# One packed pair, whole-chunk masks, fixed PSUM pools and column sums on TensorE, in a fused linear-attention and MLP kernel

## The chip, the cores and the metric

The kernel runs on one core of a Trainium2 chip. The metric is the device time of one execution in microseconds (us). Inputs and the output are float32 in the chip's main memory (HBM); products on TensorE (PE) are taken in bf16. The other engines are VectorE (DVE), ScalarE (ACT) and GpSimd (POOL); the SyncE queue (SP) issues all transfers.

## The reference, cut to what matters

A recurrence over 768 steps for 4 batches x 8 heads of 48 channels, then a two-layer MLP over all 3072 tokens:

```python
for t in range(S):                                   # S = 768
    cur = einsum('bhd,bhe->bhde', u[None] * k_t, v_t)
    y[:, :, t] = einsum('bhd,bhde->bhe', r_t, state + cur)
    state = w_t[:, :, :, None] * state + einsum('bhd,bhe->bhde', k_t, v_t)
x = y.transpose(0, 2, 1, 3).reshape(B * S, H * D)    # 3072 x 384
g = s * max(x @ w_in, 0) ** 2 + b                    # w_in 384 x 2048
out = g @ w_out                                      # w_out 2048 x 384
```

## The kernel before, in words

**Attention.** The time axis is cut into chunks of 128 steps: 6 per batch, 24 in all, numbered n = 0 to 23, in an order that takes the first two chunks of each batch first. For each chunk the steps are:

- `load` brings w, r, k and v, 192 KB each, as runs of 192 bytes (48 floats). `ln` (ACT) takes log w.
- `cum` (PE, L357) multiplies log w by triangular matrices, which gives the cumulative sums: x = 0 the exclusive ones with the chunk's whole decay in four more columns, x = 1 the negative inclusive ones. From chunk 8 on (`ONE`) only x = 0 is made, and `inc` (DVE, L416) adds log w to it. `exp` and `exn` (ACT, L411 and L426) take exponentials into E.
- `mul` (DVE, L435 or L442) gives r and k scaled by E (`prd`). `tr` and `tev` transpose them: up to chunk 8 PE transposes and ACT copies out (L469, L489, L492); from chunk 9 on a DMA transpose issued from SP does both (L499).
- `mt` (PE, L529 or L541) makes the transposed scores of each head, and `msk` (DVE, L553) multiplies them by the causal mask into bf16.
- `dmm` (PE), `sup` (DVE) and `st` (POOL) bring the 48 x 48 states forward; `l2` (POOL) spreads the decay.
- `rkp`, `rku` (POOL), `cd` (DVE, L343) and `yd` (POOL, L349) give the diagonal term with u; `vb` casts v to bf16.
- `ymm` (PE, L572 to L604) forms y from scores and state, `yev` (DVE, L649) adds the diagonal term, and `xtr` (PE) and `xev` (ACT, L712) transpose the result into xT.

**Packed pairs.** The first two chunks of a batch can be loaded as a pair: each partition then gets two neighbouring steps, in runs of 384 bytes, and each "chunk" of the pair holds every second step. Such a pair needs more, smaller matmuls (two per cumulative sum, halves of 64 rows for scores and y) and its own masks. Before, `PK = 4`: two pairs, chunks 0 to 3.

**MLP.** Two chunks make a tile of 256 tokens, T = 0 to 11. `g1` (L747) makes h in eight pieces of six matmuls per tile, `relu` (ACT, L760) and `sq` (ACT L770 or DVE L772) give the activations, `g2` (L791) multiplies by w_out, in quarters of four matmuls, for each half of the tile, `oev` (DVE, L802) scales by s and adds the bias term, and `store` (SP, L821) writes out. The weights come in four pieces each (`li`, `lo`), cast to bf16 by `ci` and `co`.

**The bias term** is b times the column sums of w_out. Before, DVE adds the float32 pieces (`csred` L829, `csadd` L836), `cssplit` (L839, L840) splits the sum into two bf16 parts, `csspread` (PE, L847) sums them over partitions with a matrix of ones, and `csevac` (ACT, L853) scales by b.

**PSUM.** There are eight banks. Six form one pool `P`, which cums, transposes, scores, states, y, xT and h share, one bank per buffer, in rotation; two belong to the o products (`o`).

**Order.** Nothing is scheduled at run time. The string `ORDER` lists every operation, and each engine runs its own in this order; `@A`, `@D` or `@P` after a name puts it on another engine, and `+16` stands for 16 warm-up products on PE (L1117). The plan (`add`) only states dependences and buffers: a buffer's next user waits until the last reader of the user before it is done. The waits themselves are made when the kernel is built. Loads, DMA transposes and stores stand in one SP queue, so an operation that waits there holds up those behind it.

Of the kernel before, what the change touches and what calls it, by code (L numbers as in the profile page):

```python
# [8 lines left out]
FP32 = mybir.dt.float32  # L9
# [13 lines left out]
WB = 5  # L23
VB = 6
PK = 4
# [13 lines left out]
load0.0 ln0 load0.1 ln1 +16 cum0.0 exp0.0 cum0.1 cum1.0 load0.2 exp0.1 exp1.0 load2.0 load_u cum1.1  # L39
load0.3 l21 load2.3 load2.1 mul0.0 mul0.1 l20 +3 tr0 exp1.1 ln2 u_mm ln3 mul1.0 cum2.0 mul1.1 tev0  # L40
u_ev tr1 exp2.0 tev1 cum2.1 vb1@A exp2.1 rkp0 vb0 rku0 cd0 +6 mt0 msk0.0 load2.2 load4.0 msk1.0
cum3.0 dmm0 li0 exp3.0 sup0 st0 msk0.1 rkp1 cum3.1 li1 msk1.1 +7 dmm1 ymm0 ymm1 vb2 exp3.1 mul2.0
mul2.1 yd0 l22 li2 mul3.0 tr2 ln4 li3 rku1 vb3 cd1 mul3.1 rkp3 cum4.0 ci0 tr3 yd1 yev0 rku3 l23 sup1
yev1 +3 dmm2 tev2 xtr0 exp4.0 tev3 xev0 xtr1 sup2 cd3 lo0 xev1 rkp2 ci1 st2 st1 +3 mt2 dmm3 msk2.0
rku2 g10.0 l24 msk2.1 lo1 msk3.0 msk3.1 g10.1 sup3 ci2 relu0.1 g10.2 sq0.1 relu0.0 lo2 small2
relu0.2 small sq0.2@A sq0.0@A ci3 g10.3 yd3 lo3 cd2 ymm3 g10.4 yev3 yd2 ymm2 co0 g10.5 g10.6 load5.0
relu0.4 yev2 g20.0 sq0.4 co1 relu0.3 xtr2 relu0.6 relu0.5 xev2 xtr3 g10.7 cum4.1 xev3 csred0 g20.4
g11.0 g11.1 sq0.6@A sq0.5@A sq0.3@A csred1 load6.0 load4.1 load4.3 load4.2 g11.2 g11.3 g20.5 load5.1
co2 csadd1@D csred2 load5.2 co3 relu0.7 relu1.0 sq0.7@A relu1.1 relu1.2 exp4.1 sq1.0@A g20.6 load6.1
load6.2 csadd2@D csred3 ln5 g11.4 g20.1 g11.5 cum5.0 sq1.2 cum5.1 g11.6 sq1.1 g20.2 ln6 csadd3@D  # L50
exp5.0 relu1.3 load5.3 cum6.1 g20.3 load7.0 cssplit relu1.4 load8.0 csspread relu1.5 exp5.1 cum6.0
g20.7 load9.0 csevac mul4 sq1.3 oev0.0 tr4 relu1.6 exp6.0 mul5 vb4 dmm4 g21.0 g21.1 exp6.1 rkp4 rku4
tr5 sup4 st4 load6.3 vb5 load7.1 tev4 oev0.1 tev5 g11.7 relu1.7 l25 rkp5 load7.2 sq1.7 sq1.5 sq1.4
load7.3 rku5 load9.3 mul6 g21.4 mt4 ln7 load8.1 cd4 msk4.0 sq1.6 msk5.0 tr6 g21.5 dmm5 msk4.1 cum7.0
g21.6 l26 yd4 msk5.1 cd5 ymm4 tev6 ln8 sup5 g21.2 yev4 cum7.1 cum8.0 yd5 inc8 ymm5 ln9 load8.2 g21.3
exp7.0 vb6 xtr4 exp8.0 exp7.1 st3 l27 yev5 cum9.0 exn8 st5 mul7 oev1.0 xtr5 xev4 vb7 xev5 exp9.0
g21.7 load10.0 inc9 dmm6 g12.0 relu2.0 load11.0 sup6 rkp6 l28 sq2.0 g12.1 relu2.1 tr7 rku6 dmm7
load9.1 g12.2 tev7 sq2.1 sup7 relu2.2 g12.3 load9.2 g12.4 mul8 sq2.2 mt6 vb9@A relu2.3 rkp7 load10.1
g22.0 g12.5 sq2.3 relu2.4 g22.1 msk6.0 msk6.1 sq2.4 msk7.0 rku7 rkp8 load8.3 load12.0 l29 cd6
relu2.5 load10.2 yd6 exn9 cd7 msk7.1 oev1.1 ln10 sq2.5 ymm6 g12.6 relu2.6 yd7 ln11 yev6 g12.7 mul9  # L60
ymm7 tr8 cum10.0 g22.4 g22.5 g22.6 rku8 xtr6 yev7 inc10 xtr7 st7 tev8 load11.3 relu2.7 exp10.0 st6
sq2.7 xev6 xev7 g22.2 dmm9 cum11.0 sq2.6@A exn10 cd8 exp11.0 load11.1 sup9 inc11 g13.0 tev9 load13.0
vb8 l210 load10.3 store0.1 store0.0 rkp9 rku9 vb11 g13.1 load13.1 g13.2 mul10 g22.7 dmm8 relu3.0
relu3.1 sq3.0@A mt8 rkp10 g22.3 relu3.2 exn11 g13.3 sup8 msk8.0 msk9.0 cd9 g13.4 yd8 st8 ln12 sq3.1
relu3.3 sq3.3 ln13 vb10@A load11.2 msk8.1 g13.5 oev2.0 ymm8 cum12.0 yd9 relu3.5 load12.1 relu3.4
msk9.1 g23.0 sq3.4@A load13.2 exp12.0 oev2.1 ymm9 sq3.5@D g13.6 g23.4 dmm10 tev10 load12.2 rkp11
yev8 g13.7 cum13.0 l211 inc12 xtr8 rku10 yev9 exn12 st9 sq3.2 xev8 xtr9 rkp13 rku11 g23.1 g23.2
relu3.6 xev9 g23.5 relu3.7 mul11 load12.3 store1.0 sq3.6@A exp13.0 g23.6 tev11 sq3.7 inc13 cd10
load13.3 store1.1 sup10 g14.0 dmm11 g14.1 g14.2 relu4.0 mul12 st10 exn13 g14.3 sup11 cd11 relu4.1
mul13 relu4.2 load14.0 g23.3 g14.4 sq4.0@A relu4.3 sq4.1 sq4.2@A rku13 relu4.4 sq4.3 mt10 g14.5  # L70
g23.7 g14.6 msk10.0 msk10.1 oev3.0 ln14 relu4.5 rkp12 g14.7 load15.1 msk11.0 tev13 tev12 msk11.1
cum14.0 vb12 l212 rku12 yd10 ymm10 g24.0 yd11 oev3.1 ymm11 relu4.6 relu4.7 yev10 inc14 dmm12 yev11
sup12 sq4.7 xtr10 g24.4 g24.1 cd12 sq4.4@D xev10 exp14.0 cd13 load16.0 l213 xtr11 load15.0 mt12
g24.5 vb13@A sq4.5 load14.1 xev11 ln15 exn14 msk12.0 load17.1 msk12.1 g15.0 g24.6 msk13.0 g15.1 yd12
load14.2 st11 msk13.1 ymm12 st12 rkp14 relu5.0 cum15.0 dmm13 load15.2 ln16 yd13 mul14 rkp15 rku14
g15.2 sq4.6 inc15 sup13 g24.2 relu5.2 load17.0 relu5.1 sq5.0 yev12 load18.1 store2.0 g15.3 g24.3
exp15.0 cum16.0 g15.4 sq5.2 ln17 exn15 ymm13 load16.1 l214 g15.5 load14.3 sq5.1 relu5.3 relu5.4
g24.7 load16.2 store2.1 oev4.0 sq5.3 l215 vb14 load17.2 rkp17 rku15 inc16 yev13 xtr12 g25.0 exp16.0
g15.6 xtr13 tev14 relu5.5 st13 l216 mul15 oev4.1 relu5.6 exn16 tev15 load17.3 xev12 xev13 cum17.0
g15.7 exp17.0 dmm14 g25.1 relu5.7 g25.4 store3.1 store3.0 load15.3 g16.0 sq5.6@A sq5.5@D inc17 g16.1  # L80
sq5.4 g25.5 g16.2 cd14 cd15 sup14 g25.2 g16.3 relu6.1 g25.6 sq5.7 l217 vb17@P load20.0 mul16 st14
rku17 yd14 yd15 exn17 rkp16 load18.0 relu6.0 mul17 load16.3 load21.1 sq6.1 load18.3 load18.2
store4.1 relu6.2 sq6.0@A load19.0 relu6.3 mt14 msk14.0 tev17 sq6.2@A g16.4 tev16 g16.5 g25.3 msk15.0
vb15 ln18 msk14.1 oev5.0 msk15.1 g16.6 relu6.6 dmm15 relu6.4 g25.7 cum18.0 ymm14 sup15 load21.0
oev5.1 sq6.4 inc18 yev14 ymm15 g26.4 yev15 relu6.5 sq6.3 exp18.0 g26.0 g26.5 exn18 xtr15 sq6.5@D
g16.7 ln19 g26.6 xtr14 dmm17 store4.0 g26.1 xev14 load20.1 xev15 load19.1 relu6.7 g26.2 sq6.6@A
# [75 lines left out]
def kernel(  # L162
# [995 lines left out]
```

## Time and profile before

| | |
|---|---|
| median of 3 runs | 198.82 us (197.65 to 199.19) |
| the profiled execution: its time, its span | 198.82 us, 197.0 us |
| granted TensorE clock, mean over the span | 0.983 |
| h products (L747), 576 matmuls | 73.4 us busy |
| o products (L791), 400 matmuls | 74.3 us busy |
| masks (L553), 48 of 128x512 | 30.8 us busy |
| r and k products (L442, L435) | 30.3 us busy |
| relu (L760), 96 of 128x512 | 54.7 us busy, 21.4 us idle before it |
| column sums on DVE (L829, L836, L839, L840) | 10.3 us busy |
| DMA queue of SP | 113426 packets, 33.83 MB, 76.6% of 16 engines' span |

Busy times are unions of what the profiler recorded. PE's matmuls are pipelined and overlap, so the time that a piece takes on PE is better read from one piece's start to the next one's. In a line of the timeline, the first number is the start in us from the span's start, the second the time covered, then engine, line, operation, output and inputs, and in brackets the idle time of that engine just before and what ended it. "PEld" is the weight load, which overlaps PE.

### The profile page before, as it was taken

Reading aid. Unit: us, or ns where it says so; the run is one execution under the profiler, and the core shown is the slowest. Engines: PE = TensorE matmul, PEld = TensorE weight load, DVE = VectorE, ACT = ScalarE, POOL = GpSimd, SP = SyncE. Lnnn points to the kernel's source line nnn. Section 1 sums busy time; section 2 is a strip of 40 time slices with the busy share of each in tenths; the row PEclk is TensorE's granted clock in tenths of the full one; section 3 lists DMA queues with packets and bytes.
Section 4 is the critical chain, followed back from the end, with each engine's and each line's share of the span. In section 5 each row is a group of like instructions: output and inputs, shape, how many; then the busy total and the mean of one; then the engine's idle time right before and its main releaser. Section 6 shows DMA issues by size and latency. Waiting matters only on the chain.

```text
span 197.0 us, 5099 instructions
## 1 busy us (share of the span) xinstructions
PE 180.9 (92%) x1994; PEld 141.6 (72%) x1994; DVE 150.1 (76%) x260; ACT 137.1 (70%) x268; POOL 110.1 (56%) x147
## 2 busy tenths in 40 slices
PE   7898699978698988999998998999999999999992
PEld 4466488855468867868876886778787777789772
DVE  7469569999788995989989878859949699533222
ACT  3682956965538959978784886588888858366730
POOL 3686970168249499866859389539459456100000
PEclk9999889999969999999999999999999999999999
DMA  6999998979997009969898998998499981020023
GB/s 155 261 259 350 403 352 261 179 154 224 214 213 150 3 7 227 171 145 195 136 210 187 223 239 173 222 224 162 79 203 236 193 189 45 0 80 5 2 78 120
DMA packets 113449, 34.14 MB, mean 173 GB/s; under 512 B 108177, under 2 KB 111378, under 8 KB 113426
## 3 DMA queue, kind: packets, MB, share of 16 engines
q1 hardware_dynamic: 113426, 33.83, 76.6%
q8 instruction: 15, 0.25, 0.5%
q14 instruction: 8, 0.07, 0.1%
HBM read 25.17 MB, written 4.72 MB: 152 GB/s over the span
## 4 chain that ended last, share of the span: by engine, by line
PE 46%; DVE 19%; DMA 8%; issue 7%; SPq 7%; POOL 7%; ACT 4%; DVEq 0%; POOLq 0%; ACTq 0%
PE o_ps L791 19%; PE h_ps L747 18%; SPq L294 5%; DVE gT L772 4%; DMA vt<-in_v_dram 4%; DVE mt_sb L553 3%; DMA u_row<-in_u_dram 2%; POOL yd L349 2%; DVE wo_st L829 2%; DVE prd L442 2%; DMA rkt<-in_k_dram 2%; ACT RK L489 2%; SPq L302 2%; PE y_ps L604 1%; POOL rkp L320 1%
## 5 line engine op out<-in xcount | busy, mean ns | idle before, releaser
L791 PE MATMUL o_ps<-w_out,gT 128*128 128x384 bf16 (+1 forms) x400 | 74.3, 323 | 1.0 <-DVE gT L772 0.8
L747 PE MATMUL h_ps<-xT,w_in 128*128 128x256 bf16 x576 | 73.4, 275 | 1.5 <-ACT xT L712 1.3
L760 ACT ACTIVATE rh<-h_ps 128x512 bf16<-128x512 f32 x96 | 54.7, 601 | 21.4 <-PE h_ps L747 20.4
L747 PEld LDWEIGHTS <-w_in 128*128 128x128 bf16 x576 | 61.8, 114 | 6.1 <-issue 1.7
L791 PEld LDWEIGHTS <-gT 128*128 128x128 bf16 x400 | 37.2, 98 | 18.8 <-DVE gT L772 1.2
L770 ACT ACTIVATE gT<-rh 128x512 bf16<-128x512 bf16 x58 | 35.8, 640 | 0.3
L326 POOL TENSOR_TENSOR rku<-rkp,u_bc 128x384 f32<-128x384 f32 x24 | 26.4, 1099 | 4.4 <-DVE cd L343 4.0
L349 POOL TENSOR_TENSOR yd<-vt,cd 128x384 bf16<-128x384 f32 x20 | 18.1, 909 | 18.9 <-DVE cd L343 18.1
L442 DVE TENSOR_TENSOR prd<-rkt,E 128x768 bf16<-128x768 f32 x20 | 25.3, 1270 | 4.1 <-DMA rkt<-in_k_dram 3.6
L320 POOL TENSOR_TENSOR rkp<-rkt 128x384 f32<-128x384 f32 x20 | 23.6, 1183 | 8.0 <-DMA rkt<-in_k_dram 8.0
L772 DVE TENSOR_TENSOR gT<-rh 128x512 bf16<-128x512 bf16 x38 | 22.4, 600 | 7.2 <-ACT rh L760 7.1
L553 DVE TENSOR_TENSOR mt_sb<-mt_ps,tri_strict 128x512 bf16<-128x512 f32 x40 | 25.7, 680 | 1.3 <-PE mt_ps L541 1.2
L802 DVE SCALAR_TENSOR_TENSOR o_sb<-o_ps,s_bc,bconst 128x384 f32<-128x384 f32 (+1 forms) x25 | 14.8, 593 | 11.5 <-PE o_ps L791 11.5
L411 ACT ACTIVATE E<-cums 128x388 f32<-128x388 f32 (+1 forms) x32 | 15.6, 498 | 11.4 <-DVE inc L416 7.0
L686 POOL TENSOR_TENSOR st<-stmp,l 128x384 bf16<-128x384 bf16 x16 | 15.2, 955 | 5.9 <-DVE stmp L677 5.9
L870 POOL CAST vb<-vt 128x384 bf16<-128x384 f32 x16 | 9.0, 567 | 12.5 <-DMA vt<-in_v_dram 12.5
L649 DVE TENSOR_TENSOR x_sb<-y_ps,yd 128x384 bf16<-128x384 f32 x24 | 13.0, 548 | 3.2 <-PE y_ps L604 1.8
L416 DVE TENSOR_TENSOR inc<-cums,logw 128x384 f32<-128x384 f32 x16 | 8.8, 550 | 6.6 <-ACT E L411 4.3
L343 DVE TENSOR_REDUCE cd<-rku 128x8 f32<-128x384 f32 x24 | 12.7, 540 | 1.5 <-POOL rku L326 1.5
L712 ACT COPY xT<-xt_ps 128x384 bf16<-128x384 bf16 x24 | 10.7, 484 | 2.7 <-PE xt_ps L697 2.7
L315 ACT ACTIVATE logw<-wt 128x384 bf16<-128x384 f32 x20 | 10.3, 527 | 2.3 <-DMA wt<-in_w_dram 2.2
L677 DVE TENSOR_TENSOR stmp<-d_ps,st 128x384 bf16<-128x384 f32 x16 | 8.8, 547 | 1.5 <-PE d_ps L636 1.0
(94 smaller groups left out, 201.8 us busy)
## 6 DMA issues: line engine op xcount, KB each, us to landing
out_dram<-o_sb SPq DMA_DIRECT2D x23, 192.0 KB, 3.0
wt<-in_w_dram SPq DMA_DIRECT2D x20, 192.0 KB, 3.8
rkt<-in_r_dram SPq DMA_DIRECT2D x20, 192.0 KB, 4.0
vt<-in_v_dram SPq DMA_DIRECT2D x20, 192.0 KB, 3.6
rkt<-in_k_dram SPq DMA_DIRECT2D x20, 192.0 KB, 3.9
wi_st<-in_moe_w_in_dram SPq DMA_DIRECT2D x4, 768.0 KB, 8.0
wo_st<-in_moe_w_out_dram SPq DMA_DIRECT2D x4, 768.0 KB, 6.3
pkt<-in_w_dram SPq DMA_DIRECT2D x2, 384.0 KB, 4.8
```

Source lines behind the costliest of these rows:

```text
L320: nc.gpsimd.tensor_tensor(out=rkp, in0=c["r"], in1=c["k"], op=ALU.mult)
L326: nc.gpsimd.tensor_tensor(out=rku.rearrange("t h d -> t (h d)"), in0=c["rkp"].rearrange("t h d -> t (h d)"), in1=u_bc, op=ALU.mult,)
L349: nc.gpsimd.tensor_tensor(out=yd, in0=c["v"], in1=c["cd"].unsqueeze(2).to_broadcast([128, H, D]), op=ALU.mult,)
L411: nc.scalar.activation(out=c["E"][:, x, 0:w], in_=ps[:, 0:w], func=AF.Exp)
L442: nc.vector.tensor_tensor(out=prd[:, :, :, 0:D], in0=c["rk"], in1=c["E"][:, :, 0:HD].rearrange("t x (h d) -> t x h d", h=H), op=ALU.mult,)
L553: nc.vector.tensor_tensor(out=c["mt"][:, sg], in0=c["mt_ps"][sg], in1=(masks[:, n % 2] if packed(n) else tri_strict) .unsqueeze(1) .to_bro ...
L686: nc.gpsimd.tensor_tensor(out=c["st_new"], in0=c["stmp"].rearrange("q p (g e) -> q p g e", g=2), in1=c["l2"].unsqueeze(3).to_broadcast([12 ...
L747: nc.tensor.matmul(ps[:, f, :], lhsT=w_in_sb[ft // FPP][:, kt, :].rearrange("p (m j) -> p j m", j=FPP)[:, ft % FPP, :], rhs=xT[T][:, kt, : ...
L760: nc.scalar.activation(out=rh, in_=hs[T, i], func=AF.Relu)
L770: nc.scalar.activation(out=g, in_=rh, func=AF.Square)
L772: nc.vector.tensor_tensor(out=g, in0=rh, in1=rh, op=ALU.mult)
L791: nc.tensor.matmul(os_[T, k][:, cols], lhsT=gT[T][:, ft, tt * 128 : (tt + 1) * 128], rhs=w_out_sb[ft // FPP][:, ft % FPP, cols], start=(ft ...
```

## The change

It replaces the order string and, with it, five things:

1. `PK = 2`: one packed pair (chunks 0 and 1). Chunks 2 and 3 are loaded and computed like the rest; with one pair, the chunk order is batch 0's first two, then the first chunks of batches 1 to 3, then their second chunks, and so on. The packed transposes get two buffers (`RK2`).
2. PSUM: pool `P` is cut into `A`, one buffer of two banks for cums and scores; `B`, two buffers of one bank for transposes, states, y, xT and the column sums; and `h`, two of one bank. The pool `o` stays.
3. Both halves of a chunk's cumulative sum form one operation in one `A` buffer, read by one wide exponential and, up to chunk 7, a small one for the decay.
4. Scores and masks: one `mt` and one `msk` of 1024 columns per chunk, where there was one `mt` per two chunks and four `msk` of 512 columns. The masked scores have three buffers instead of four.
5. Column sums: 48 matmuls with one column of ones (`colsum`) add up w_out's bf16 pieces in a `B` buffer; DVE splits 128x3 values, and six matmuls spread them. The float32 pieces' staging buffers come free after their cast.

In the order, warm-up products are 74 instead of 38; four squares and five casts of v more are on ACT; of the w_in casts, piece 1 goes from POOL to ACT and piece 2 from ACT to DVE; load_u is third; and the loads of r and k for chunk 4 stand between the w_out pieces. The words that name the change speak of padded tiles; the padded tiles are in both kernels, but for `cs_sum`, which is 128x2x16 and used in three columns. `mul` of a packed chunk becomes one operation of two instructions.

```diff
-PK = 4
+PK = 2
-    psP = ctx.enter_context(
-        tc.tile_pool(name="psP", bufs=6, space=bass.MemoryType.PSUM)
+    psA = ctx.enter_context(
+        tc.tile_pool(name="psA", bufs=1, space=bass.MemoryType.PSUM)
     )
+    psB = ctx.enter_context(
+        tc.tile_pool(name="psB", bufs=2, space=bass.MemoryType.PSUM)
+    )
+    psH = ctx.enter_context(
+        tc.tile_pool(name="psH", bufs=2, space=bass.MemoryType.PSUM)
+    )
...
-    def cum(n, x):
+    def cum(n):
+        ps = psA.tile([128, 2, 512], FP32, name="cums", tag="A")
...
+        if n < ONE:
+            nc.scalar.activation(out=E[:, :, 0:HD], in_=ps[:, :, 0:HD], func=AF.Exp)
+            if cc < NCH - 1:
+                nc.scalar.activation(
+                    out=c["lam"], in_=ps[:, 0, HD : HD + HP], func=AF.Exp
+                )
+            return
...
     def mt(n):
-        two = [n, n + 1]
...
+        ps = psA.tile([128, 2, HP, 128], FP32, name="mt_ps", tag="A")
...
+    def mask(n):
+        m = work.tile([128, 2, HP, 128], BF16, name="mt_sb", tag="mt_sb")
         nc.vector.tensor_tensor(
-            out=c["mt"][:, sg],
-            in0=c["mt_ps"][sg],
+            out=m.rearrange("s g p t -> s (g p) t"),
+            in0=c["mt_ps"].rearrange("s g p t -> s (g p) t"),
...
-        ps = psP.tile([128, FPQ, TOK], FP32, name="h_ps", tag="P")
+        ps = psH.tile([128, FPQ, TOK], FP32, name="h_ps", tag="h")
...
-    def csred(i):
...
+    def colsum(i):
+        if i == 0:
+            os_["cs"] = psB.tile([128, 512], FP32, name="cs_ps", tag="B")
+        for ft in range(i * FPP, (i + 1) * FPP):
+            for kt in range(KT):
+                nc.tensor.matmul(
+                    os_["cs"][:, kt : kt + 1],
+                    lhsT=w_out_sb[i][:, ft % FPP, kt * 128 : (kt + 1) * 128],
+                    rhs=ones[:, 0:1],
+                    start=(ft == 0 and kt == 0),
+                    stop=(ft == FT - 1 and kt == KT - 1),
+                )
...
-        dict(w=WB, rk=8, v=VB, lw=NLW, prd=NPR, E=2, RK=RKB, M=MB, vb=6, yd=6, x=XSB, RK2=1,
-             cd=4, rkp=2, rku=2, l2=5, P=6, o=2, gT=3, xT=XTB, rh=4, inc=1,
+        dict(w=WB, rk=8, v=VB, lw=NLW, prd=NPR, E=2, RK=RKB, M=3, vb=6, yd=6, x=XSB,
+             cd=4, rkp=2, rku=2, l2=5, A=1, B=2, h=2, o=2, gT=3, xT=XTB, rh=4, inc=1,
```

The start of the new order, up to the first h product:

```text
load0.0 load0.1 load_u load0.2 load2.0 ln0 ln1 load2.1 +18 cum0 load2.2 u_mm exp0 load0.3 +2 cum1
l20 mul0 li0 exp1 rkp1 u_ev +1 tr0 load3.1 ln2 mul1 tev0 load3.2 +6 cum2 rku1 +2 tr1 exp2 load2.3
...
xtr0 yev1 xev0 +3 cum3 cd2 rku3 dmm2 xtr1 exp3 load4.0 sup2 +6 dmm1 xev1 mul3 lo0 ci1@A +2 ymm2
g10.0
```

## The prediction

> **What bounds the kernel now.** I read the whole span first (the page), then a table of five stretches, then waits and the order of time in each. The stretches are cut where TensorE's order changes: its first h product at 24.8 us, the first h product of tile 2 (g12.0) at 60.8, the last attention product at 166, the last matmul at 193.5.
>
> ```profile
> PE 180.9 (92%) x1994; PEld 141.6 (72%) x1994; DVE 150.1 (76%) x260; ACT 137.1 (70%) x268; POOL 110.1 (56%) x147
> ```
> ```profile
> core 0: us, PE busy (x) PEld busy (x) DVE busy (x) ACT busy (x) POOL busy (x), PEclk, DMA share, GB/s
> 0.00:24.80 24.80, 20.23 (x300) 13.78 (x300) 16.65 (x42) 15.12 (x24) 17.55 (x37) 0.96 1.06 287
> 24.80:60.80 36.00, 32.01 (x344) 24.06 (x344) 31.35 (x50) 23.10 (x46) 16.18 (x21) 0.93 0.95 221
> 60.80:166.00 105.20, 101.15 (x1112) 81.65 (x1112) 90.85 (x148) 83.45 (x170) 75.56 (x90) 1.00 0.83 168
> 166.00:193.50 27.50, 27.48 (x243) 22.08 (x240) 10.87 (x22) 15.42 (x30) 0.83 (x1) 1.00 0.10 36
> 193.50:197.00 3.50, 0.00 (x0) 0.00 (x0) 0.42 (x1) 0.00 (x0) 0.00 (x0) 1.00 0.35 123
> ```
>
> Until 24.8 loads and short chains bound it (DMA share 1.06). From 24.8 to 60.8 PE loses 4.0 us idle, and its clock is 0.93. From 60.8 on it is TensorE: 4.0 us idle in 105, none in the tail. To count losses I give each piece of PE work its start-to-start time when nothing waits: an h product of six matmuls 0.656 us (18 in 1.97 in the chain), an o quarter 0.65, and per chunk cum 0.27, score products 0.275, y 0.53, state 0.17, the x transpose 0.33, the transposes of r and k 0.45 where PE makes them. In the written order these sum to 29.5 us from the first h product to g12.0, and took 36.0: 6.5 lost. From there to the last matmul they sum to 131.8 and took 132.7: 0.9 lost. So the long stage has nothing to win on PE, and whatever makes PE wait there adds to the time.
>
> The waits of PE inside the second stretch, in order of time:
>
> ```profile
> 44.62 0.34 PE L847 MATMUL csb_ps<-cs_sum,ones 128*128 128x384 bf16 x1 [1.34 <-DVE cs_sum L839]
> 45.21 0.32 PE L847 MATMUL csb_ps<-cs_sum,ones 128*128 128x384 bf16 x1 [0.25 <-DVE cs_sum L840]
> ...
> 52.78 0.62 PE L469 MATMUL trps<-identity,prd 128*128 128x128 bf16 x8 [1.75 <-DVE prd L442]
> ```
>
> Two belong to the column sums, which leave; the third is the chain of chunk 6. The chain of waits runs through loads just before:
>
> ```profile
> 43.87 1.06 SPq L294
> ...
> 46.78 0.70 SPq L294
> 47.53 3.55 DMA vt<-in_v_dram
> ```
>
> Last, how long a result stays in PSUM until it is read out. The line with L541 makes the scores of chunks 8 and 9, the next three mask them; then a cumulative sum (L389) and its two readers:
>
> ```profile
> 78.06 0.62 PE L541 MATMUL mt_ps<-RK 48*128 48x128 bf16 x16
> ```
> ```profile
> 79.07 1.27 DVE L553 TENSOR_TENSOR mt_sb<-mt_ps,tri_strict 128x512 bf16<-128x512 f32 x2
> 80.72 0.68 DVE L553 TENSOR_TENSOR mt_sb<-mt_ps,tri_strict 128x512 bf16<-128x512 f32 x1
> 81.84 0.68 DVE L553 TENSOR_TENSOR mt_sb<-mt_ps,tri_strict 128x512 bf16<-128x512 f32 x1
> ```
> ```profile
> 85.13 0.33 PE L389 MATMUL cums<-logw,tri_strict 128*128 128x384 bf16 x1
> ```
> ```profile
> 88.00 0.52 ACT L411 ACTIVATE E<-cums 128x388 f32<-128x388 f32 x1
> ```
> ```profile
> 88.54 0.56 DVE L416 TENSOR_TENSOR inc<-cums,logw 128x384 f32<-128x384 f32 x1 [0.86 <-ACT E L411]
> ```
>
> The cumulative sum is held from 85.13 to 89.1, 4.0 us; over chunks 9 to 23 the hold is 1.6 to 4.2 us, mean 3.1. The first mask starts 0.4 to 2.7 us after the scores do (mean of ten pairs 1.14), and two masks take 1.36, so a chunk's scores are held about 2.5 us, 4.06 at the most. Before, six shared banks take this up. After, cums and mt_ps share one double bank, "A", used twice per chunk: 3.1 + 2.5 = 5.6 us of the 5.8 us that a chunk takes in the third stretch (105.2 us for 18 chunks).
>
> **The change part by part.** The profiled execution has a span of 197.0 us and a time of 198.82, 1.8 more, which is also the median of the three runs; I add 1.8 to spans. The padding that the change names stands in both kernels: what moves is everything else in the diff.
>
> 1. One packed pair instead of two. Loads: four of 384 KB go, eight of 192 KB come. In the busy queue packed loads are issued every 1.48 us (7.21, 8.70, 10.18), unpacked ones every 1.01 (25 from 36.10 to 61.37): 8 x 1.01 - 4 x 1.48 = +2.2 us of queue time. From the eight loads issued between 42.24 and 49.29 alone (0.88 each) it is +1.1. I take 2.2, the longer sample. It lies ahead of chunk 4 to 7's loads, which the chain runs through. The Trainium skill, "DMA: Bandwidth & Descriptors", sections "Why small descriptors are slow (HBM only)" and "How a descriptor splits into AXI transactions", counts beats of 32 B plus about 3 cycles per packet: 9 for a run of 192 B, 15 to 18 for one of 384. By it (an estimate) a packed load of 1.48 us becomes two of 0.74 to 0.89, and the price is 0 to 1.2 us, not 2.2; the time below would then be 201.6 to 202.8.
>
> 2. PE work. Up to the first h product the idle PE has warm-up products to spare (74 instead of 38, 0.11 us each); these cost only where they stand before ready work. From g10.0 to g12.0 the pieces sum to 30.3 instead of 29.5: two packed y products leave (0.92 each), chunk 3's front part comes in, and the column sums bring 48 one-column matmuls. Eight such (L378) take 0.29 us, four (L395) 0.10, so 1.2 to 1.7, taken 1.4. From g12.0 on it is 132.5 instead of 131.8, one o quarter more.
>
> 3. Column sums leave VectorE: eleven adds, a cast and a subtraction, 10.3 us busy between 32.8 and 45.2. Most lay beside a PE busy all of 30 to 40; the two waits above, 1.6 us, go. Their cover was missing only there.
>
> 4. Masks: 24 of 1024 columns for 48 of 512. From 384 columns (0.548) to 512 (0.68) a column costs 1.03 ns, so one takes 0.68 + 0.53 = 1.21 instead of 1.36; bounds 0.95 (a 768-column product at its shortest) and 1.36. VectorE gets 3.6 us lighter; beside a PE-bound stage that is worth nothing by itself. Four squares and five casts of v move to ACT (4 x 0.64 + 5 x 0.51 = 5.1 us); ACT is idle 60 us, so 0.
>
> 5. Start, walked along the new order. Both halves of cum0 come before exp0: 6.7 instead of 6.3. The u product now stands before cum1 on PE; u is loaded third, at about 1.9, and if it takes 4.8 us as now, PE is through it at 7.6. Then cum1 8.6, exp1 9.6, ln2 10.1, tev0 11.1, exp2 12.1, tev1 13.1, mt0 13.6 (now 12.95). With one buffer the masks go in turn: mask 0 to 15.0, mt1 15.5, mask 1 16.9, mt2 and cd0, mask 2 18.8, yev0 19.3, xtr0 19.7, xev0 20.3, exp3 21.3, xev1 21.8. The first h product starts at 21.8 instead of 24.8, because only chunk 2 goes ahead of it rather than a second packed pair, and because ACT no longer waits for the first weights ahead of tev2 (2.9 us idle at 16.4). Bounds: 19.8 (no u wait, no buffer turns) and 25 (the walk's waits on loads as long as now). Step: -3.0.
>
> 6. PSUM. For each use of A in the new order I take the PE work between the end of one user and the start of the next, 32 uses from g12.0 on, and compare it with the holds above less the piece's own PE time (2.8 after a cum, 2.2 after scores). Nine fall short, by 3.6 us in all, and 0.3 before g12.0. With the shortest holds (1.5 and 1.6 after the piece) none falls short: 0. With the longest everywhere (3.9 and 3.8) the sum is 27.4. The two "B" buffers (y, d, trps, xt; holds y 1.9, d 1.8 in the mean) fall short by 1.6 before g12.0 and 1.2 after. For h (two buffers) the work between a product and the next but one is never under 1.0 us; nine times it is 1.0 to 1.4, and a relu of 0.60 with its semaphores fits: 0 to 3.6, taken 0. After g12.0 I take 4.0 for A, B and h together, not 4.8, since a wait for A gives B its time too. That is nearest to the mean holds, which the same engines at nearly the same load will repeat. The Trainium skill, "Perfetto Trace Analysis", section "Matmuls", says that independent matmul groups should rotate through PSUM banks so that the read-out of one overlaps the next; by that rule a one-buffer A exposes the read-out at every use, which from these holds would be nearer the 27.4 than the 3.6, and the time as much as 227.
>
> Sum: first h product at 21.8; pieces 30.3; losses 6.5 - 1.6 + 2.2 + 1.6 + 0.3 = 9.0; g12.0 at 61.1, +0.3 against now. Then +0.7 of pieces and +4.0 of PSUM waits: 197.0 + 5.0 = 202.0, time **203.8 us**.
>
> **The rivals.** A, faster: the gain at the start is kept. For it: VectorE is 10 us lighter while it was on the chain, and the new order brings chunk 4's k ahead of two of the weight pieces. Without the 2.2 and the B waits g12.0 comes at 21.8 + 30.3 + 4.9 = 57.0, 3.8 early, and with no PSUM waits the end is 197.0 - 3.8 + 0.7 = 193.9, time 195.7. It decides where g12.0 is before 58 us and the waits after it are under 2 us. Against: the holds. B, no change: the start as in my sum, short holds later (0 to 2): 197.0 + 0.3 + 0.7 + 1 = 199.0, time 200.8 at its upper edge; with 1.1 for the loads 199.7. C, much slower: A is the bound. For it: 5.6 of 5.8 us. Halfway between the mean and the longest holds (15.5 in place of 3.6) the time is 203.8 + 11.9 = 215.7; a third of the way, 207.8. Against: the order was laid out for these gaps, and PE waits slow the work that crowds VectorE. That the change does little is part of B: PE work differs by 1.5 us only.
>
> **How the numbers follow.** Forecast (200.8 to 208) 0.50, A 0.18, B 0.19, C above 208 0.13. Within 1% is about what a measurement of this kernel can tell from no change. Faster 0.18, same 0.19, slower 0.63. The range leaves a tenth on each side: 196.5, above A's 195.7, to 210, in C's near part. The likeliest case's own range is 200.8 to 208.
>
> **What would show it.** The first h product near 21.8; g12.0 near 61; PE waits, named by exp, inc or mask, in front of cum and mt after it, some 3 to 5 us; no PE wait for relu over 0.5 us; the bias product with no wait for VectorE. Wrong would be: g12.0 before 58 (A), idle PE over 10 us after it (C), or PE waits for DMA.

## The result and the profile after

| | before | after |
|---|---|---|
| median | 198.73 us (4 runs, 197.65 to 199.19) | 188.09 us (4 runs, 187.63 to 188.47) |
| profiled execution: time, span | 198.82, 197.0 | 188.43, 186.7 |
| granted clock, mean | 0.983 | 0.999 |
| first h product (g10.0), that of tile 2 (g12.0) | 24.79, 60.83 | 22.13, 53.46 |

The ratio of the times is 0.947 (95% interval 0.942 to 0.952): 10.6 us faster, where 203.8 was forecast. First the line of the page with busy time by engine, then the same five stretches, cut at the same places of the order:

```profile
PE 180.7 (97%) x1994; PEld 142.3 (76%) x1994; DVE 131.7 (71%) x220; ACT 142.0 (76%) x277; POOL 104.5 (56%) x141
```
```profile
core 0: us, PE busy (x) PEld busy (x) DVE busy (x) ACT busy (x) POOL busy (x), PEclk, DMA share, GB/s
0.00:22.10 22.10, 20.86 (x281) 14.79 (x282) 16.04 (x36) 13.31 (x23) 15.48 (x32) 1.00 0.94 247
22.10:53.40 31.30, 30.20 (x367) 23.76 (x362) 23.09 (x38) 26.46 (x51) 16.02 (x21) 1.00 0.99 252
53.40:155.00 101.60, 101.60 (x1098) 81.46 (x1093) 80.62 (x126) 85.84 (x176) 68.72 (x85) 1.00 0.93 189
155.00:183.20 28.20, 28.03 (x266) 22.30 (x263) 11.66 (x23) 16.35 (x31) 4.24 (x5) 1.00 0.14 45
183.20:186.70 3.50, 0.00 (x0) 0.00 (x0) 0.28 (x1) 0.00 (x0) 0.00 (x0) 0.94 0.26 85
```

TensorE's busy time is the same (180.9 and 180.7 us); what went is the time in which it had nothing to do, and some clock. The span lost 10.3 us: 2.7 ahead of g10.0; 4.7 from there to g12.0 (36.0 became 31.3: 2.9 less idle, and 1.8 less busy time with the clock at 1.00 instead of 0.93); 3.1 from g12.0 to the last matmul (132.7 became 129.6); the tail behind it is 0.2 longer. In the third stretch PE is busy 101.60 of 101.60 us. The same program run again (after_again) had g12.0 at 52.54, so a microsecond there is scatter. All of PE's waits in the whole kernel fit in three lines (total, times, longest):

```profile
PE warm_ps L1110 <- DVE warm_sb L1067: 1.1, 1, 1.1
PE trps L478 <- DVE prd L451: 0.8, 2, 0.5
PE h_ps L749 <- POOL w_in L881: 0.2, 1, 0.2
```

Before, the same view of the long stage (60.8 to 194) had 4.5 us; these are the five largest of seven lines:

```profile
PE h_ps L747 <- ACT xT L712: 1.3, 2, 0.8
PE o_ps L791 <- DVE gT L772: 0.8, 2, 0.6
PE d_ps L636 <- POOL vb L870: 0.8, 1, 0.8
PE y_ps L604 <- DVE mt_sb L553: 0.6, 1, 0.6
PE y_ps L595 <- DVE mt_sb L553: 0.5, 1, 0.5
```

The bias product, for which PE waited 1.6 us before, now starts 0.4 us after the second of its two small inputs is done. On the first lines VectorE reads 128x3 values where it read 128x384:

```profile
41.76 0.15 DVE L844 CAST cs_sum<-cs_ps 128x3 bf16<-128x3 f32 x1
41.95 0.16 DVE L846 TENSOR_TENSOR cs_sum<-cs_ps,cs_sum 128x3 bf16<-128x3 f32 x1
42.50 0.50 PE L854 MATMUL csb_ps<-identity,cs_sum 128*128 128x128 bf16 x6
44.19 0.96 DVE L451 TENSOR_TENSOR prd<-rkt,E 128x768 bf16<-128x768 f32 x1 [2.08 <-DMA rkt<-in_k_dram]
```

The last line matters most: VectorE is idle for 2.08 us and takes chunk 5's product the moment its k has landed. Before, VectorE had no gap that the trace shows from 31.09 to 49.49 us; here is the middle of that row of work:

```profile
40.01 3.02 DVE L829 TENSOR_TENSOR wo_st<-wo_st 128x768 f32<-128x768 f32 x2
42.95 0.75 DVE L772 TENSOR_TENSOR gT<-rh 128x512 bf16<-128x512 bf16 x2
43.62 0.55 DVE L836 TENSOR_TENSOR wo_st<-wo_st 128x384 f32<-128x384 f32 x1
44.20 0.36 DVE L839 CAST cs_sum<-wo_st 128x384 bf16<-128x384 f32 x1
44.60 0.56 DVE L840 TENSOR_TENSOR cs_sum<-wo_st,cs_sum 128x384 bf16<-128x384 f32 x1
45.07 0.95 DVE L442 TENSOR_TENSOR prd<-rkt,E 128x768 bf16<-128x768 f32 x1
45.94 0.72 DVE L772 TENSOR_TENSOR gT<-rh 128x512 bf16<-128x512 bf16 x1
```

Last, the holds of "A": the scores of a chunk and their mask, then a cumulative sum and its two readers.

```profile
78.02 0.40 PE L544 MATMUL mt_ps<-RK 48*128 48x128 bf16 x8
78.48 1.22 DVE L555 TENSOR_TENSOR mt_sb<-mt_ps,tri_strict 128x1024 bf16<-128x1024 f32 x1
83.26 0.33 PE L388 MATMUL cums<-logw,tri_strict 128*128 128x384 bf16 x1
83.80 0.50 ACT L419 ACTIVATE E<-cums 128x388 f32<-128x388 f32 x1
84.34 0.56 DVE L424 TENSOR_TENSOR inc<-cums,logw 128x384 f32<-128x384 f32 x1 [0.33 <-ACT E L419]
```

The mask follows its scores at once: the buffer is held 1.7 us here, 1.83 in the mean of chunks 8 to 23. The cumulative sum is held 1.6 us here, 2.2 in the mean. From the holds before I had put 2.5 and 3.1.

### The profile page after: what moved, and what is told of

Same layout as the page of the kernel before. It is cut to its first block, busy times and chain, and to the rows that moved or that the text cites. A ratio compares the mean times of both kernels' runs of the same rounds, so it can differ in the third digit from the quotient of the medians.

```text
span 186.7 us, 5073 instructions
## 1 busy us (share of the span) xinstructions
PE 180.7 (97%) x1994; PEld 142.3 (76%) x1994; DVE 131.7 (71%) x220; ACT 142.0 (76%) x277; POOL 104.5 (56%) x141
## 3 DMA queue, kind: packets, MB, share of 16 engines
q1 hardware_dynamic: 117586, 33.83, 80.3%
## 4 chain that ended last, share of the span: by engine, by line
PE 82%; DMA 8%; SPq 4%; DVE 2%; issue 1%; ACT 0%; DVEq 0%
PE o_ps L793 31%; PE h_ps L749 29%; DMA wo_st<-in_moe_w_out_dram 6%; PE warm_ps L1110 4%; PE mt_ps L544 4%; SPq L297 3%; DMA rkt<-in_k_dram 2%; PE y_ps L607 2%; PE xt_ps L700 2%; PE y_ps L598 2%; PE trps L478 2%; PE cums L388 2%; PE d_ps L639 1%; PE cums L373 1%; DVE gT L774 1%
## 5 line engine op out<-in xcount | busy, mean ns | idle before, releaser
L749 PE MATMUL h_ps<-xT,w_in 128*128 128x256 bf16 x576 | 77.6, 274 | 0.2 <-POOL w_in L881 0.2
L762 ACT ACTIVATE rh<-h_ps 128x512 bf16<-128x512 f32 x96 | 56.5, 598 | 14.9 <-PE h_ps L749 13.4
L793 PEld LDWEIGHTS <-gT 128*128 128x128 bf16 x400 | 36.2, 98 | 15.3
L352 POOL TENSOR_TENSOR yd<-vt,cd 128x384 bf16<-128x384 f32 x22 | 20.0, 917 | 27.3 <-DVE cd L346 23.4
L555 DVE TENSOR_TENSOR mt_sb<-mt_ps,tri_strict 128x1024 bf16<-128x1024 f32 x22 | 26.8, 1220 | 4.3 <-PE mt_ps L544 4.0
L451 DVE TENSOR_TENSOR prd<-rkt,E 128x768 bf16<-128x768 f32 x22 | 22.9, 1039 | 3.0 <-DMA rkt<-in_k_dram 2.1
L652 DVE TENSOR_TENSOR x_sb<-y_ps,yd 128x384 bf16<-128x384 f32 x24 | 13.2, 554 | 11.5 <-PE y_ps L607 10.6
L774 DVE TENSOR_TENSOR gT<-rh 128x512 bf16<-128x512 bf16 x34 | 16.0, 488 | 4.9 <-ACT rh L762 4.9
L689 POOL TENSOR_TENSOR st<-stmp,l 128x384 bf16<-128x384 bf16 x16 | 13.1, 825 | 1.1 <-DVE stmp L680 1.1
L1110 PE MATMUL warm_ps<-warm_sb 128*128 128x256 bf16 x74 | 12.2, 309 | 1.1 <-DVE warm_sb L1067 1.1
L881 POOL CAST vb<-vt 128x384 bf16<-128x384 f32 x14 | 7.4, 536 | 6.8 <-DMA vt<-in_v_dram 6.8
L465 POOL TENSOR_TENSOR l<-E,par 128x8 f32<-128x8 f32 x20 | 7.0, 352 | 6.7 <-ACT E L419 4.7
```

The lines of the kernel that those rows point to most:

```text
L352: nc.gpsimd.tensor_tensor(out=yd, in0=c["v"], in1=c["cd"].unsqueeze(2).to_broadcast([128, H, D]), op=ALU.mult,)
L451: nc.vector.tensor_tensor(out=prd[:, :, :, 0:D], in0=c["rk"], in1=c["E"][:, :, 0:HD].rearrange("t x (h d) -> t x h d", h=H), op=ALU.mult,)
L555: nc.vector.tensor_tensor(out=m.rearrange("s g p t -> s (g p) t"), in0=c["mt_ps"].rearrange("s g p t -> s (g p) t"), in1=(masks[n % 2] if ...
L749: nc.tensor.matmul(ps[:, f, :], lhsT=w_in_sb[ft // FPP][:, kt, :].rearrange("p (m j) -> p j m", j=FPP)[:, ft % FPP, :], rhs=xT[T][:, kt, : ...
L762: nc.scalar.activation(out=rh, in_=hs[T, i], func=AF.Relu)
L774: nc.vector.tensor_tensor(out=g, in0=rh, in1=rh, op=ALU.mult)
```

## The experiments

Four theories were open after the result. **V**: VectorE was the bound of the stretch from g10.0 to g12.0, and taking the column sums off it is the gain. **P**: the second packed pair, dropped, is the gain. **M**: the PSUM pools and the wide masks are. **O**: how long a PSUM buffer is held follows from the written order, not from the engines. **C**, a lesser one: gaps that warm-up products would fill lower the granted clock. A sixth, **L**, came up on the way: where the buffers stand in SBUF. The kernel before was run beside each batch; its medians were 197.6 to 199.1 us.

### b_colsum_pe: the order before, column sums on TensorE

```diff
-csred0 .. csred3, csadd1@D .. csadd3@D        (VectorE, spread over the order)
+colsum0 colsum1 colsum2 colsum3 cssplit       (48 matmuls, together)
-    cs_sum = const.tile([128, 2, d_model], BF16, ...)
+    cs_sum = const.tile([128, 2, 16], BF16, ...)[:, :, 0:KT]
```

> The kernel before, with one part of the change: the column sums of w_out come from 48 one-column matmuls, made together just ahead of their split, and the eleven VectorE additions leave. Theory O (the written order sets PE's waits; the parts alone do little): 197 to 199 us, with PE waits elsewhere in 40 to 61 us and g12.0 still after 58 us. Theory V (the 10.3 us of VectorE work at 32.8 to 45.2 held up the attention of chunks 4 and 5): 193 to 195.5 us, g12.0 at 56 us or earlier.

Measured: 193.63 us, ratio 0.985 (0.977 to 0.994); g12.0 at 55.64. That is V's forecast, and just under half of the change's gain. The trace then showed something that V can't explain: the first h product was at 21.55 instead of 24.79, long before the first column sum. The edit had done a second thing, which b_pad64 and b_cs_1536 below take apart.

### b_pk2: the order before, one packed pair

```diff
-PK = 4
+PK = 2        # chunks 2 and 3 loaded and computed singly
```

> The kernel before, with one part of the change: one packed pair instead of two, the loads of chunk 3 right after those of chunk 2, the rest of the order as it was. Theory O: 197 to 200 us; the first h product 0 to 2 us earlier, and taken back before g12.0. Theory P (the second packed pair costs the time): 194 to 196 us, the first h product near 22 us and g12.0 3 us earlier or more.

Measured: 201.42 us, ratio 1.022 (1.014 to 1.031), slower than either theory forecast, and g10.0 was not earlier but 0.4 us later (25.15). P falls for this order. PE's four largest waits, up to g12.0 at 63.85:

```profile
PE mt_ps L469 <- ACT RK L420: 2.8, 2, 1.9
PE csb_ps L775 <- DVE cs_sum L767: 2.4, 1, 2.4
PE trps L397 <- DVE prd L370: 1.7, 1, 1.7
PE csb_ps L775 <- DVE cs_sum L768: 1.1, 1, 1.1
```

The single chunks' transposes come late for their scores, and the bias product waits longer for VectorE than before (3.5 us in place of 1.6).

### a_colsum_dve: the order after, column sums on VectorE

```diff
-colsum0 / colsum1 / colsum2 / colsum3
+csred0 / csred1 csadd1@D / csred2 csadd2@D / csred3 csadd3@D
-    cs_sum = const.tile([128, 2, 16], BF16, ...)[:, :, 0:KT]
+    cs_sum = const.tile([128, 2, d_model], BF16, ...)
```

> The changed kernel with one part undone: the column sums are VectorE additions again, at the places in the order where the matmuls stood. Theory O: 188 to 190 us, since VectorE has room between the transfers of the weight pieces (3.8 us idle for them) and PE loses at most 2 us. Theory V: 191.5 to 195 us, with PE waiting for mul or mask of chunks 4 and 5 before g12.0.

Measured: 197.54 us, ratio to before 1.000 (0.996 to 1.005): nearly the whole gain is gone, 9.4 us of it, more than V forecast. (The tile of the packed transposes also went back to one buffer, of which a single pair needs no more.) Its g10.0 is where it was (22.18); g12.0 is at 61.48 instead of 53.46.

```profile
core 0: us, PE busy (x) PEld busy (x) DVE busy (x) ACT busy (x) POOL busy (x), PEclk, DMA share, GB/s
0.00:22.10 22.10, 20.84 (x280) 14.76 (x280) 15.98 (x36) 13.37 (x23) 15.47 (x32) 1.00 1.01 240
22.10:61.40 39.30, 30.99 (x316) 23.11 (x312) 34.29 (x48) 26.55 (x50) 17.34 (x22) 0.96 0.89 227
```
```profile
PE csb_ps L780 <- DVE cs_sum L772: 4.1, 1, 4.1
PE o_ps L724 <- DVE w_out L805: 2.7, 3, 1.8
...
PE trps L408 <- DVE prd L381: 0.9, 1, 0.9
```

VectorE is busy 34.29 of 39.30 us (23.09 of 31.30 in the kernel after), and what PE waits for is whatever stands behind the sums in VectorE's order: casts of w_out (2.7 us), then the sums' end (4.1). Chunk 5's product starts at 49.49 instead of 44.19:

```profile
48.62 0.36 DVE L772 CAST cs_sum<-wo_st 128x384 bf16<-128x384 f32 x1
49.01 0.56 DVE L773 TENSOR_TENSOR cs_sum<-wo_st,cs_sum 128x384 bf16<-128x384 f32 x1
49.49 0.95 DVE L381 TENSOR_TENSOR prd<-rkt,E 128x768 bf16<-128x768 f32 x1
```

After g12.0 this kernel has no wait of PE either, as the kernel after. So the gain of the long stage isn't the column sums'. The 9 us are the price of the sums where the matmuls stood in this order; other places for them were not tried.

### a_pool4c: the order after, four shared banks instead of the fixed pools

```diff
-    psA: 1 buffer of two banks; psB: 2 of one
+    psP: 4 buffers of one bank, for all of them
-one mask of 1024 columns, one exponential of 768
+two masks of 512, two exponentials of 384
```

The column sums stand together ahead of cssplit here.

> The changed kernel with one part undone: scores and cumulative sums lie in single banks that they share with the B tiles (four in rotation), with two masks of 512 columns and two exponentials of 384 per chunk; the column sums' matmuls stand together ahead of their split. Theory O: 187.5 to 189.5 us; VectorE 3 us busier, PE waits under 1.5 us. Theory M (the wide masks and own buffers bring the gain): 191 to 194 us, with PE waits for masks after g12.0.

Measured: 187.5 us, ratio 0.954 (0.946 to 0.962); PE waits 0.3 us, beside the first warm-up's 1.1 that every version has. M falls: in this order neither the fixed pools nor the wide masks bring anything. Five more rounds on one chip gave 187.67 for it and 187.64 for the kernel after, and 188.18 for the kernel after with only the column sums moved together: no version found is better than the change as it stands.

> The kernel after with four single banks in rotation in place of the fixed pools, 512-column masks, and the column sums together, once more, beside the kernel after on the same chip. It was 187.5 against 188.1 us, inside the spread. If the pools bring nothing: within 1 us of the kernel after. If the rotation is really better: 0.6 us or more below it.

> The kernel after with only the place of the column sums changed: all 48 matmuls together ahead of their split, instead of four groups of twelve between o and h products. If the groups' places matter (a matmul that waits for a cast of w_out holds up PE): up to 0.6 us faster. If not: within 0.5 us of the kernel after.

> The kernel after itself, unchanged, as the common yardstick on this chip for the two runs above: 187.6 to 188.5 us.

### a_mask_late and a_hold1: who sets the holds

The first moves masks alone; the second adds 16 copies of 512 columns of scores ahead of masks, into a tile that the mask then overwrites.

```diff
-mt8 relu3.3 g13.4 msk8 ...
+mt8 relu3.3 g13.4 ... msk8      # as late as the next use of A allows, from chunk 8 on
```
```diff
+nc.vector.tensor_copy(out=m[:, 0], in_=ps[:, 0])     # ahead of 16 masks
```

> The changed kernel with one thing moved: each mask from chunk 8 on stands as late on VectorE as the next use of its buffer allows, behind 0 to 3 other operations (23 in all). Same work, longer holds of the A buffer. Theory O (holds, and so waits, follow from the order): scores held 2.5 us or more in the mean instead of 1.8, PE waits for VectorE in front of cum and scores of 3 to 8 us, 190 to 195 us. The other theory (PE's queue runs so far ahead of nothing that a later mask is hidden): 188 to 189 us.

> The changed kernel with an additional VectorE copy of 512 columns of the scores, overwritten afterwards, ahead of each mask from chunk 8 on: 16 of 0.6 us, 10 us more VectorE work in the long stage and a hold of the A buffer longer by 0.6 us, the order as it is. If VectorE's load is what the kernel before suffered from: 192 to 196 us, PE waits over 4 us. Theory O: the order leaves room, 188 to 190 us.

Measured: 193.22 us (ratio to before 0.976, 0.969 to 0.983), 5.1 more than the kernel after, with the same instructions; and 190.4 (0.961, 0.953 to 0.969), 2.3 more and just above O's range, with 11 us more of VectorE work (142.9 busy). The late masks bring waits for masks. Half of them are of the kind that I had forecast, a cumulative sum that waits for its buffer; the other half are y products that wait for their masked scores:

```profile
PE y_ps L537 <- DVE mt_sb L485: 2.0, 2, 1.0
PE cums L318 <- DVE mt_sb L485: 1.9, 2, 1.3
```

O holds for the masks: put behind other operations, 23 in all, they cost more than 11 us of added work on their engine. With that work VectorE is busy 103.4 us after g12.0, as in the kernel before (101.7), but PE is idle there for 0.6 us and not for 4.0; the rest of the 2.3 us is mostly PE work that takes 1.2 us longer, for which no run gives a cause. Nor is it the mean hold: the scores are held 2.7 us in the mean with late masks and 2.6 with the copies (1.8 in the kernel after). It matters where in the order a long hold falls.

### b_warm57, a_warm35 and b_cs_warm: warm-ups and the clock

```diff
 b_warm57, b_cs_warm
-st2 st1 +3 mt2
+st2 st1 +22 mt2
 a_warm35
-+6 cum2 / +14 mt0 / +13 mt2 / +6 dmm1
+cum2 / mt0 / mt2 / dmm1
```

> The kernel before with 19 more warm-up products in the gap of PE ahead of the second packed scores (22 instead of 3). Theory C (the clock granted at 0.81 to 0.85 in 20 to 30 us cost part of the time): the clock back at 1.00 there and 0.8 to 2 us less, 196.7 to 198. Otherwise: 198 to 199, since PE waits later for the same chains.

> The changed kernel without 39 of its 74 warm-up products (those ahead of cum2, mt0, mt2 and dmm1). Theory C: a lower granted clock between 10 and 30 us and 190 to 193 us. Otherwise: 188 to 188.6 us, and nothing changes after the first h product.

> The kernel before with both edits at once: column sums as 48 matmuls, standing together ahead of their split, and 19 more warm-up products ahead of the second packed scores. Alone they brought 4.6 us and about 1.5 us. If the two losses are separate (one is VectorE at 32 to 50 us, one is the clock at 20 to 25 us), they add: 192 to 193 us, the first product of tile 2 at about 54 us. If the warm-ups and the freed VectorE removed the same gap, it stays at 193.6, within 0.5 us. If the padding, pools and masks of the change were needed for the rest, nothing of that kind can bring it under 190.

Measured: 197.44 us (195.29 to 202.58; ratio 0.991, 0.985 to 0.997), 191.06 (0.965, 0.951 to 0.978) and 195.91 (0.990, 0.984 to 0.995; neither of its forecasts). Without its 39 warm-ups the kernel after is 3.0 us slower in the median of four runs (189.5, 189.9, 192.3, 193.8), 1.8 without the slowest. The granted clock, without them and then with them, in the same two stretches:

```profile
10.00:20.00 10.00, 7.45 (x157) 5.58 (x156) 8.38 (x12) 6.79 (x11) 8.39 (x11) 0.92 0.96 261
20.00:30.00 10.00, 9.54 (x117) 8.38 (x116) 8.54 (x14) 8.86 (x16) 4.83 (x6) 0.91 1.05 346
```
```profile
10.00:20.00 10.00, 9.87 (x186) 7.51 (x184) 8.06 (x12) 6.80 (x11) 8.04 (x11) 1.00 0.97 256
20.00:30.00 10.00, 9.71 (x124) 8.48 (x123) 8.10 (x14) 9.10 (x17) 5.29 (x6) 1.00 1.04 312
```

In the order before, 19 warm-ups ahead of the second packed scores fill a wait of 2.0 us and help a little; the run scatters too much to say how much. Added to b_colsum_pe they did harm: 2.3 us in the medians, though the intervals of the two ratios overlap (0.984 to 0.994 is in both). The trace shows 1.6 of it: the scores' input is ready at 20.58, the warm-ups stand before them, and they start at 22.09 instead of 20.53. A filler is free only while the wait that it fills is there.

### b_pad64, b_cs_1536, a_pad64, a_csdve_pad: the place of the buffers and the column sums, apart

Making cs_sum 1472 bytes smaller moves every buffer allocated behind it. By the sizes of the tiles ahead of them, added up from the first, the load buffers begin 64 bytes past a multiple of 128 in the kernel before and at a multiple of 128 in the kernel after. One unused tile undoes or makes that, for the load buffers and for all others behind it:

```diff
 b_pad64, a_pad64, a_csdve_pad
     cs_sum = ...
+    pad = const.tile([128, 16], FP32, name="pad", tag="pad")      # 64 bytes
 b_cs_1536: b_colsum_pe with
-    cs_sum = const.tile([128, 2, 16], BF16, ...)[:, :, 0:KT]
+    cs_sum = const.tile([128, 2, d_model], BF16, ...)[:, :, 0:KT]
```

> The kernel before with one unused 128x16 float32 tile after cs_sum: every SBUF buffer behind it moves up by 64 bytes and nothing else changes. The traces so far split by where the load buffers begin: at 64 bytes past a multiple of 128 the packed loads ran at 261 GB/s from 4 to 15 us (before, with 19 warm-ups more, with one pair), at a multiple of 128 at 325 GB/s (after, and both of mine with a small cs_sum). Theory L (place in SBUF): 325 GB/s, first h product at about 21.6 instead of 24.8, clock 1.0, time 195 to 196.5. Theory V (VectorE's column sums are all of it): 198.6, as before, with the first h product at 24.8.

> The kernel before with column sums on TensorE, as in the earlier run, but with cs_sum left at its 1536 bytes, so that no buffer moves. That run took 193.6 us with the buffers 64 bytes further on. If the column sums alone made the 5 us: 193.6. If the place of the buffers made the part ahead of the first h product (2.5 to 3.2 us): the loads are back at 261 GB/s, the first h product at 24.8, and the time is 196 to 196.5; then the column sums are worth 2 to 2.5 us and the place the rest.

> The kernel after with one unused 128x16 float32 tile after cs_sum, which puts the load buffers at 64 past a multiple of 128, as in the kernel before. Theory L: slower loads at the start, first h product 1 us or more late at most (one packed pair only, and the run with column sums on VectorE had this place and still 22.18 there); 188 to 190. If the place matters to the later loads and to VectorE's products too (mean 1039 ns after, 1270 before): 190 us or more. Theory V: 188, no change.

> The kernel after with column sums on VectorE, as in the earlier run (197.5 us), now with one unused tile of 64 bytes after cs_sum, so that the load buffers stand where they do in the kernel after. If all of that run's 9 us was VectorE: 197.5 still. If part was the place: faster by that part, which the run before this one in the list gives from the other side (the two should add to about 9).

Measured, median time, then g10.0 and g12.0 of the profiled execution:

| | sums on VectorE | sums on TensorE |
|---|---|---|
| order before, buffers at 64 | 197.6 to 199.1 (before), 24.79, 60.83 | 195.83 (b_cs_1536), 23.32, 58.08 |
| order before, buffers at 128 | 196.15 (b_pad64), 21.61, 58.45 | 193.63 (b_colsum_pe), 21.55, 55.64 |
| order after, buffers at 64 | 197.54 (a_colsum_dve), 22.18, 61.48 | 188.45 (a_pad64), 22.27, 52.45 |
| order after, buffers at 128 | 196.64 (a_csdve_pad), 22.05, 61.14 | 188.09 (after), 22.13, 53.46 |

In the order before, the place is worth 2.4 us at g12.0 in either column and the column sums 2.8 in either row. That they come out so even is in part luck. No column sum runs before g10.0, and the programs of before and b_cs_1536 do not differ up to there; yet b_cs_1536 reaches it 1.5 us sooner, since its first weights came sooner:

```profile
19.31 1.47 ACT L868 CAST w_in<-wi_st 128x1536 bf16<-128x1536 f32 x1 [2.86 <-DMA wi_st<-in_moe_w_in_dram]
17.89 1.47 ACT L804 CAST w_in<-wi_st 128x1536 bf16<-128x1536 f32 x1 [1.43 <-DMA wi_st<-in_moe_w_in_dram]
```

So much do single executions scatter. By stretch, the sums are worth 1.3 and 2.8 us between g10.0 and g12.0, and the place 1.8 and 3.2 ahead of g10.0. (As times alone, the intervals of b_pad64, 0.992 to 1.001, and b_cs_1536, 0.989 to 1.001, just take in no change, in a batch where the kernel before spread from 195.5 to 202.4; what tells them from it are the loads, below, and PE's waits for the sums, 2.7 us in b_pad64 and 0.3 in b_cs_1536.) In the order after the place is worth no more than the scatter, 1 us, and the column sums 8 to 9.

Theory L can be read from the loads. Two packed loads in the queue of the kernel before, and what the DMA engines moved, in 40 slices from 3 to 20 us:

```profile
7.21 1.45 SPq L302 DMA_DIRECT2D pkt<-in_r_dram  x1
8.70 1.44 SPq L302 DMA_DIRECT2D pkt<-in_k_dram  x1
```
```profile
GB/s 328 321 292 261 259 263 262 261 261 261 262 261 261 261 261 262 260 261 260 262 262 259 260 262 263 255 245 255 278 318 347 366 381 328 371 352 366 366 390 414
```

The same with 64 bytes of padding and no other change (b_pad64):

```profile
6.55 1.15 SPq L303 DMA_DIRECT2D pkt<-in_r_dram  x1
7.75 1.15 SPq L303 DMA_DIRECT2D pkt<-in_k_dram  x1
```
```profile
GB/s 326 323 328 317 321 321 324 321 332 321 326 323 325 325 328 323 325 324 324 327 321 273 273 346 386 376 323 289 318 347 347 333 323 395 381 395 347 337 333 390
```

325 GB/s instead of 261, and ACT casts the first weights at 16.87 instead of 19.31. Those weights are what ACT waited for ahead of the second pair's transposes, so g10.0 comes at 21.61 instead of 24.79. With one pair only (the order after) nothing on the path waits there: a_pad64 still has 22.27.

### a_pad32 and b_pk2_pad: the border, and one pair at the better place

```diff
 a_pad32
+    pad = const.tile([128, 8], FP32, name="pad", tag="pad")       # 32 bytes
 b_pk2_pad: b_pk2 with the 64 bytes
```

> The kernel after with one unused 128x8 float32 tile after cs_sum: the load buffers and all others behind it begin 32 bytes past a multiple of 64, which is what the words of the change speak against. Moving them by 64 cost 0.4 us here and 2.4 in the old order, all of it ahead of the first h product. If only whole 128-byte lines matter to the packed loads: like the run at 64, 188 to 189. If 64 is a border of its own, for the 192-byte runs as well: slower loads all along (under 250 GB/s where the queue is busy) and 190 us or more.

> The kernel before with one packed pair, as in the earlier run (201.4 us), and the load buffers 64 bytes further on. If the 3 us that the second pair's going cost were slow packed loads: back to 198 or less. If they come from where the old order puts the single loads and the transposes: about 1 us faster than that run (half of what the place gave with two pairs), 200 to 200.5, with the waits for the transposes' copies still there.

Measured: 190.65 us (ratio to before 0.964, 0.957 to 0.971), 2.6 more than the kernel after; and 199.26 (1.008, 1.005 to 1.011). Off a multiple of 64 the single loads of w, r, k and v are slower too: the queue's packets take 88.4% of 16 engines' span where they took 80.3%, and the median single load of k lands after 4.4 us instead of 3.7 (81.0% and 3.8 in a_pad64). The large loads of w_in are not (7.3 us, 7.6 in the kernel after); those of w_out took 8.2 and 7.4. So by these runs 64 bytes is a border for the single loads, and 128 one for the packed ones (a_pad32 moves the other engines' tiles by 32 bytes as well; their part was not tried). One pair less costs 3.1 us at this place and 3.2 at the other: in the old order it is not the place that makes it slower, and P stays fallen there.

## Why the prediction was wrong, point by point

**The whole.** The span came out 15.3 us shorter than forecast: 7.6 of it before g12.0 and 7.8 from there to the last matmul.

**The start: right.** g10.0 was forecast at 21.8 and came at 22.13. The walk along the order was right in its parts, within 0.9 us: the first scores were done at 13.3 (13.6 forecast), the third mask at 18.6 (18.8), and one mask of 1024 columns takes 1.22 us (1.21).

**Column sums: the step that failed.** I wrote: "Most lay beside a PE busy all of 30 to 40; the two waits above, 1.6 us, go. Their cover was missing only there." A busy PE was taken for cover. But VectorE, at 31.35 of 36.00 us, was a bound of that stretch too, without a gap for 18 us, and each of its later operations (chunk 5's and 6's products, the outputs) came later by what stood before it. I priced the sums by what waited for the sums. The price is what waits for anything behind them, and it depends on the order: 1.3 to 2.8 us in the order before, 8 to 9 in the order after. In the order before VectorE was not the only bound: without the sums (b_colsum_pe, b_cs_1536) it is busy 22 us, and the stretch still takes 34.1 to 34.8.

**Losses that I kept.** From g10.0 to g12.0 I forecast 9.0 us of losses, 4.9 of them kept from the 6.5 before as given. Measured were 1.0: 31.3 us against 30.3 of pieces. PE was idle 1.1 us, and the clock was 1.00. The clock's part hung on the wait ahead of the second pair's scores at least in b_warm57: with that wait filled, and the sums still on VectorE, the clock was 1.00 and the stretch took 34.8 us instead of 36.0, although PE was idle 4.9. That the idle time was a consequence of VectorE's backlog is shown for the order after (1.1 us without the sums, 8.3 with them), and only in part for the order before (4.0, and 2.6 in b_cs_1536). The 2.2 us for smaller loads did not show either, though the queue has 4160 more packets, nor did the 1.9 for A and B.

**The long stage: the step failed in its carry-over.** "The mean holds, which the same engines at nearly the same load will repeat": they did not (1.83 and 2.17 us in the mean instead of 2.5 and 3.1), since the new order writes each mask right behind its scores. 4.0 us of PSUM waits were forecast; there was none. The working from means fails as well: in a_hold1 the scores are held 2.6 us, about as long as I forecast (the cumulative sums stay at 2.2), and PE waits 0.2 us for them after g12.0. Against the start-to-start times that I had used, 132.5, the stage took 129.6: those pitches were some 3 us too long, and so hid that before, too, PE lost about 4 us there, of which I saw 0.9. The Trainium skill ("Perfetto Trace Analysis", section "Matmuls") wants independent matmul groups to rotate through banks, so that the read-out of one overlaps the next. I took it to mean that a one-buffer A shows its read-out at every use, and that the runs do not bear out: one fixed buffer and four in rotation took 188.1 and 187.5 us. Between two uses of A the order has products for the other banks (B, h, o), and PE had no gap in the third stretch, so the overlap was there.

**The padding.** I wrote that it "stands in both kernels". The tile cs_sum does not, and 1472 bytes less there moved all buffers behind it. In the order before that is 2.4 us at g12.0 (1.8 to 3.2 at g10.0); in the order after it adds at most 1. The Trainium skill ("DMA: Bandwidth & Descriptors", section "How a descriptor splits into AXI transactions") lets transactions start only at multiples of 256 bytes, with what lies below fetched for nothing. It says so of reads and not of the SBUF side. If it held there too, a run of 384 bytes would take 14 beats in the mean at the better place and 16 at the other, 1.14 times as long (an estimate from that page). The measured pitch of packed loads is 1.45 us against 1.15, 1.26 times, more than that.

**The rivals.** A, faster, was the right side and by its own test: g12.0 before 58 us and the waits after it under 2 us. It had 18%, still kept 4.9 us of losses, and at 195.7 us was 7.6 too slow. In C, 207.8 us is a sixth of the way from the mean holds to the longest, not a third.

**What stays open.** From b_colsum_pe to the kernel after there are 5.5 us more. Of the 4.6 us between their two profiled executions 2.2 lie before g12.0 and 2.5 in PE's waits after it (in the old order's variants PE is busy 128.3 to 128.7 of some 132 us there, in the new one all of the 129.6). In the new order pools and mask width bring nothing, and the place is the same in the two kernels. One packed pair costs time in the old order; whether the new order needs it was not tried. So by exclusion it is the new order of the instructions, with its one pair. Two of its parts were undone: 39 warm-ups (1.8 to 3.0 us) and masks close behind their scores (5.1). They can't be added up, and the other moves were not tried.

## What to carry to other kernels

Look for an engine that has hardly a gap in its timeline over a stretch (here VectorE, 87% busy with the sums in either order), even when TensorE looks just as busy: an operation on it delays whatever stands behind it in its order, and taking it off can be worth far more than the waits that name it (1.6 us named; 1.3 to 2.8 in one order, 8 to 9 in the other). A hold of a buffer belongs to the written order; walk it in the new order instead of carrying a mean over. When a tile's size changes, look at where the tiles behind it now begin, and when an experiment changes a tile, keep its size or pad it, or it tests two things. Compare two executions of the same instructions before you split a gain by single traces: here they differed by up to 1.5 us.

## What the runs showed of the hardware

- 384-byte runs went into SBUF at 325 GB/s when the buffers began at a multiple of 128 bytes and at 261 GB/s 64 bytes past one. At 32 past a multiple of 64, single loads of k (192-byte runs) took 4.4 us to land, and 3.7 and 3.8 at the two other places.
- In some executions where TensorE waited in turns the granted clock fell: 0.92 and 0.91 from 10 to 30 us without warm-ups, 0.96 over 39 us with the column sums on VectorE, 1.00 in these stretches of the kernel after. Not in all: in b_warm57 TensorE was idle 4.9 of 34.8 us at 1.00.
- 48 matmuls with a single column did the work of 10.3 us of VectorE adds; each group of twelve covers 0.44 us on PE.
